# A tail of the first K block on a second DMA queue, and half as many wo rows for the first five DMA engines

## The chip, the cores and the metric

One core of a Trainium2 chip runs the whole kernel. The metric is the device time in microseconds (us) of one execution; medians are given with their range. The **span** of a profile runs from the first to the last instruction and is some 1.8 us shorter than the time of the same run.

## The reference

Attention of 4 new tokens in each of 8 sequences over a cache of 2048 keys, with 32 query heads and 8 key/value heads, between two projections:

```python
B, Sq, D = 8, 4, 512;  Hq, Hkv, Sk, Dh = 32, 8, 2048, 128
q = (x @ wq).reshape(B, Sq, Hq, Dh) ...
scores = einsum("bhqd,bhkd->bhqk", q, repeat(k_cache, 4)) * Dh ** -0.5
o = einsum("bhqk,bhkd->bhqd", softmax(scores), repeat(v_cache, 4))
return o... @ wo                       # everything bf16
```

K and V caches are 32 MB each, wq and wo 4 MB each: every byte is read once, so the kernel streams some 75.5 MB.

## The kernel before

The cache is cut into 32 units of 1 MB for K and 32 for V. All loads go on the sync queue, in the order K block 0, wq, x, then K and V blocks, with eight small loads of wo rows strewn in, and the rest of wo last.

```python
def load_k(u):
    ...
    nc.sync.dma_start(ks[u][:, :, :],
        k_cache[b, 2 * p : 2 * p + 2].rearrange("g (s c) d -> (g s) c d", c=C))   # 128 rows of 8 KB

NE, WE, WM, WN = 40, 8, 5, 64          # wo rows of the first 1024: NE*WE + 128*WM + WN

def load_wo_e(i):                      # five partitions x 8 rows of wo (8 KB each), i = 0..7
    ...
    nc.sync.dma_start(wo_e[a : a + 17 : 4, :, :], rows[b : b + 17 : 4, :, :])

load_k(0)
nc.sync.dma_start(wq_sb[:, :, :], wq.rearrange("(p r) n -> p r n", r=R))         # 128 rows of 32 KB
nc.sync.dma_start(x_sb[:, :], x.flatten_outer_dims())
loads = []
for u in range(NU + KA):
    if 1 <= u <= 8:
        loads.append(("e", u - 1))     # a five-row wo load between two K blocks
    if 0 < u < NU:
        loads.append(("k", u))
    ...                                # "v" blocks; wo_m and wo_n near the end
```

A load of five rows runs on five DMA engines alone (engines 0 to 4, by the rule that the prediction below cites). That looks intended: 320 wo rows are ballast for these engines. Why they should need it, the trace doesn't tell, since its packet records don't name the engine. The program's tool chain gives each DMA a semaphore on which its landing is counted; there are eight of them, used over and over.

The softmax here doesn't subtract the row's maximum and nothing guards it: scores larger than these inputs give would overflow.

## Time and profile before

| | before |
|---|---|
| time, median of 3 (range) | 188.69 us (188.62 to 189.28) |
| span of the profiled run | 186.8 us |
| bytes on the sync queue, share of 16 DMA engines | 75.55 MB, 96.5% |
| busy: PE, DVE, ACT | 77%, 71%, 33% |
| wq's packets | 4.98 to 14.83 us |

How to read it: a row of digits is the busy share of each fortieth of the span in tenths, `DMA` the mean over the 16 DMA engines and `GB/s` what they moved. An issue line of the timeline gives start and duration of the instruction that *hands out* a transfer; the transfer itself comes later. "Landing" is the increment of the transfer's semaphore, one for each DMA engine that takes part, so 16 landing records of one load tell how far the engines are apart. A load on fewer engines has one record more, soon after its issue: the first wo_e load, issued at 4.26 us, has one at 5.50 and five at 15.47 to 15.63.

### The profile page before, as it was taken

The numbers are of one execution on the slowest core, as the hardware profiler recorded it, in microseconds if no ns is written. First come the engines' busy times: TensorE is split into PE (matmuls) and PEld (weight loads), VectorE is DVE, ScalarE is ACT, GpSimd is POOL, SyncE is SP. The second block draws the span as 40 slices with busy tenths as digits, with TensorE's granted clock in tenths as the row PEclk, the third lists the DMA queues.
The fourth block names the chain that finished last, engine by engine and source line by source line (L and its number), as shares of the span: only waits on it lengthen the run. The fifth ranks groups of instructions, "written<-read, shape, count | busy, mean of one in ns | idle before, by whom it ended". The sixth has DMA issues, their size and how long they took to land.

```text
span 186.8 us, 4854 instructions
## 1 busy us (share of the span) xinstructions
PE 143.7 (77%) x2090; PEld 115.0 (62%) x2090; DVE 131.9 (71%) x260; ACT 62.4 (33%) x110; POOL 4.6 (2%) x9
## 2 busy tenths in 40 slices
PE   0704789979989969999687878977676787987592
PEld 0701248867777757887666656866565666776471
DVE  0850278979797888888786873988686887798220
ACT  2021147344535343343333331533333332335000
POOL 8100000000000000000000000000000000000000
PEclk9999999999999999999999996999999998799659
DMA  5998999999999999999999999999999999999980
GB/s 198 475 449 372 423 437 428 419 423 421 432 423 423 425 430 426 418 428 428 430 418 426 428 421 423 425 423 428 425 428 421 426 421 432 425 422 404 417 315 11
DMA packets 10980, 75.86 MB, mean 406 GB/s; under 512 B 1288, under 2 KB 1448, under 8 KB 2600
## 3 DMA queue, kind: packets, MB, share of 16 engines
q1 hardware_dynamic: 10912, 75.55, 96.5%
q8 instruction: 16, 0.26, 0.5%
q14 instruction: 4, 0.03, 0.0%
q10 hardware_dynamic: 48, 0.02, 0.0%
HBM read 75.53 MB, written 0.03 MB: 405 GB/s over the span
## 4 chain that ended last, share of the span: by engine, by line
DMA 96%; PE 1%; SPq 0%; issue 0%; ACT 0%
DMA k_sb<-in_k_cache_dram 58%; DMA v_sb<-in_v_cache_dram 26%; DMA wq_sb<-in_wq_dram 8%; DMA wo_sb<-in_wo_dram 4%; PE kp L215 1%; SPq L118 0%; PE s_ps L286 0%; PE out_ps L480 0%; ACT out_sb L545 0%; SPq L128 0%
## 5 line engine op out<-in xcount | busy, mean ns | idle before, releaser
L215 PE MATMUL kp<-ident,k_sb 128*128 128x128 f32 x512 | 73.1, 291 | 22.5 <-DMA k_sb<-in_k_cache_dram 22.3
L215 PEld LDWEIGHTS kp<-ident,k_sb 128*128 128x128 f32 x512 | 59.5, 149 | 33.2 <-issue 18.9
L216 DVE COPY kt<-kp 128x1024 bf16<-128x1024 bf16 x96 | 63.0, 686 | 22.7 <-PE kp L215 22.4
L306 DVE STREAM_TRANSPOSE probs<-s_sb 64x512 bf16<-64x512 bf16 x64 | 44.9, 702 | 0.6
L296 ACT ACTIVATE s_sb<-s_ps 128x512 bf16<-128x512 f32 x32 | 19.1, 597 | 66.7 <-PE s_ps L286 65.2
L216 ACT COPY kt<-kp 128x1024 bf16<-128x1024 bf16 x32 | 32.4, 1012 | 16.3 <-PE kp L215 16.3
L343 PE MATMUL o_ps<-probs,v_sb 128*128 128x32 bf16 x640 | 19.2, 177 | 3.2 <-DMA v_sb<-in_v_cache_dram 2.2
L343 PEld LDWEIGHTS <-v_sb 128*128 128x128 bf16 x640 | 18.6, 96 | 4.3 <-DMA v_sb<-in_v_cache_dram 3.9
L286 PE MATMUL s_ps<-kt,q_bd 128*32 128x256 bf16 x512 | 21.2, 283 | 0.0
L286 PEld LDWEIGHTS <-q_bd 128*32 128x32 bf16 x512 | 10.8, 96 | 6.0 <-issue 4.7
L381 PE MATMUL o_ps<-v_sb,probs 128*64 128x256 bf16 x192 | 11.6, 274 | 0.0
L381 PEld LDWEIGHTS <-probs 128*64 128x64 bf16 x192 | 10.0, 110 | 0.9 <-issue 0.8
L401 ACT ACTIVATE o_sb<-o_ps,r_sb 128x256 f32<-128x256 f32 x6 | 2.8, 474 | 12.4 <-DVE r_sb L399 12.4
L354 DVE TENSOR_TENSOR oT<-o_ps,r_sb 128x32 bf16<-128x32 f32 x20 | 3.8, 191 | 3.6 <-PE o_ps L343 3.0
L296 ACT ACTIVATION_READ_ACCUMULATOR s_sb<-s_ps 128x1 f32 x32 | 6.2, 194 | 0.0
L336 DVE RECIPROCAL r_sb<-l_ps 128x64 f32<-128x64 f32 x10 | 5.6, 557 | 0.3
L410 PE MATMUL f_ps<-fold,o_sb 128*128 128x64 f32 x24 | 4.0, 287 | 2.4 <-ACT o_sb L401 2.4
L480 PE MATMUL out_ps<-wo_sb,oP 128*32 128x256 bf16 x48 | 5.0, 342 | 0.5 <-DMA wo_sb<-in_wo_dram 0.5
L252 DVE COPY qT_all<-qtp 128x128 bf16<-128x128 bf16 x8 | 1.2, 217 | 5.8 <-PE qtp L246 5.8
L410 PEld LDWEIGHTS f_ps<-fold,o_sb 128*128 128x128 f32 x24 | 3.1, 190 | 3.6 <-ACT o_sb L401 3.3
L227 PE MATMUL xtp<-ident,x_sb 32*128 32x32 bf16 x4 | 0.3, 194 | 6.3 <-DMA x_sb<-in_x_dram 6.3
L243 ACT ACTIVATE q_nat<-psq 128x512 bf16<-128x512 f32 x2 | 1.2, 597 | 10.4 <-PE psq L236 10.4
(59 smaller groups left out, 64.1 us busy)
## 6 DMA issues: line engine op xcount, KB each, us to landing
k_sb<-in_k_cache_dram SPq DMA_DIRECT2D x32, 1024.0 KB, 19.6
v_sb<-in_v_cache_dram SPq DMA_DIRECT2D x32, 1024.0 KB, 12.6
wq_sb<-in_wq_dram SPq DMA_DIRECT2D x1, 4096.0 KB
wo_sb<-in_wo_dram SPq DMA_DIRECT2D x4, 512.0 KB
wo_sb<-in_wo_dram SPq DMA_DIRECT2D x4, 256.0 KB, 9.3
wo_m<-in_wo_dram SPq DMA_DIRECT2D x1, 640.0 KB, 16.7
wo_e<-in_wo_dram SPq DMA_DIRECT2D x8, 40.0 KB
wo_n<-in_wo_dram SPq DMA_DIRECT2D x1, 64.0 KB
```

The lines of the kernel that those rows point to most:

```text
L215: nc.tensor.transpose(kp[:, j, :], k4[:, w : w + 128], ident4[:, :])
L216: (nc.scalar.copy if part == 3 else nc.vector.tensor_copy)(out=kt[(u, t)][:, half * JT // 2 : (half + 1) * JT // 2, :, :].rearrange("k j s ...
L286: nc.tensor.matmul(s_ps[y * 32 : (y + 1) * 32, t * JT : (t + 1) * JT, :], lhsT=q_bd[:, p, e, b, y // 2, :, :], rhs=kt[(u, t)][:, :, y * 32 ...
L296: nc.scalar.activation(out=s_sb[:, :, :], in_=s_ps[:, :, :], func=EXP, accum_out=l_sbs[u][:, u % 2 : u % 2 + 1],)
L306: nc.vector.transpose(out=pr[rows, :, g, :], in_=s_sbs[u][rows, :, :].rearrange("q j s -> q (j s)"))
L336: nc.vector.reciprocal(r_sb[:, :, :], l_ps[:, :, :])
L343: nc.tensor.matmul(o_ps[:, :], lhsT=vs[u][:, c, :], rhs=pr[:, c, :, :].rearrange("s g q -> s (g q)"), start=(c == 0), stop=(c == C - 1),)
L354: nc.vector.tensor_tensor(out=oT[(p + 1) // 2][:, :, (p == 2) * 1, b, :], in0=o_pss[u][:, :].rearrange("d (h s) -> d h s", h=HP), in1=r_sb ...
L381: nc.tensor.matmul(o_ps[i * 64 : (i + 1) * 64, :], lhsT=probs[(u + i) % len(probs)][:, c : c + 2, :, :].rearrange("s c g q -> s (c g q)"), ...
L401: nc.scalar.mul(out=o_sb[:, :, :].rearrange("q c d -> q (c d)"), in_=o_ps[:, :], mul=r_sb[:, 0:1])
L410: nc.tensor.matmul(f_ps[:, :, :].rearrange("d u q -> d (u q)"), lhsT=o_sbs[u][:, c, :], rhs=fold[:, c, :, :].rearrange("k u q -> k (u q)") ...
L480: nc.tensor.matmul(out_ps[half * T : (half + 1) * T, :], lhsT=o, rhs=w[:, half * DH : (half + 1) * DH], start=(p == 0 and r == 0), stop=(p ...
```

## The change

Two things are meant to make the sixteen DMA engines end together. First, 160 instead of 320 rows of wo go through the first five engines (four loads instead of eight); wo_m grows from 5 to 6 rows per partition and wo_n from 64 to 96 rows. Second, the last two of the 32 chunks of K block 0 (512 B in each of 128 rows) leave the first K load and go on the scalar queue in sixteen small loads of 15, 14, ... 1 and 8 rows. By the rule that the prediction cites, a load of k rows (k up to 15) uses the first k engines, so engine 0 gets 16 rows, engine 1 fifteen, and engine 15 none: a fine slope.

```diff
-    NE, WE, WM, WN = 40, 8, 5, 64
+    NE, WE, WM, WN = 20, 8, 6, 96
...
-        nc.sync.dma_start(
-            ks[u][:, :, :],
-            k_cache[b, 2 * p : 2 * p + 2].rearrange("g (s c) d -> (g s) c d", c=C),
-        )
+        rows = k_cache[b, 2 * p : 2 * p + 2].rearrange("g (s c) d -> (g s) c d", c=C)
+        if u > 0:
+            nc.sync.dma_start(ks[u][:, :, :], rows)
+            return
+        nc.sync.dma_start(ks[u][:, : C - 2, :], rows[:, : C - 2, :])
+        a = 0
+        for k in [*range(15, 0, -1), 8]:
+            nc.scalar.dma_start(ks[u][a : a + k, C - 2 :, :], rows[a : a + k, C - 2 :, :])
+            a += k
...
-        hi, m = divmod(i, 4)
         rows = wo[: NE * WE, :].rearrange("(q r) j -> q r j", r=WE)
-        a, b = hi * 32 + m, hi * NE // 2 + m
-        nc.sync.dma_start(wo_e[a : a + 17 : 4, :, :], rows[b : b + 17 : 4, :, :])
+        nc.sync.dma_start(wo_e[i : i + 17 : 4, :, :], rows[i : i + 17 : 4, :, :])
...
-        if 1 <= u <= 8:
+        if 1 <= u <= 4:
```

The cut parts give wo_e 32 partitions instead of 64, one copy fewer on DVE in the reordering of the outputs, and one more row of wo_m in the projection.

More of the change, by code (lines that the diff above doesn't have):

```diff
@@ L74 @@
     pad0 = const.tile([128, 192], BF16, name="pad0")
-    wo_e = const.tile([64, WE, D], BF16, name="wo_e")
+    wo_e = const.tile([32, WE, D], BF16, name="wo_e")
     wo_n = const.tile([WN, D], BF16, name="wo_n")
@@ L92 @@
     oP12 = const.tile([128, WR, 2, T], BF16, name="oP12")
-    nat_sb = const.tile([2 * T, HP * 128 + 24 * WE], BF16, name="nat_sb")
+    nat_sb = const.tile([2 * T, HP * 128 + 12 * WE], BF16, name="nat_sb")
     oP3 = const.tile([128, WR, T], BF16, name="oP3")
     oP = [None, oP12[:, :, 0, :], oP12[:, :, 1, :], oP3[:, :, :]]
-    oE = const.tile([64, WE, T], BF16, name="oE")
+    oE = const.tile([32, WE, T], BF16, name="oE")
     oM = const.tile([128, WM, T], BF16, name="oM")
@@ L105 @@
     ones = const.tile([128, 128], FP32, name="ones")
-    pad = const.tile([128, 64], BF16, name="pad")
+    pad = const.tile([128, 128], BF16, name="pad")
     probs = [const.tile([128, C, 2, HQ], BF16, name=f"probs{i}") for i in range(3)]
@@ L431, in to_tokens @@
         flat = nat[:, :, :].rearrange("t h d -> t (h d)")
-        nats[n] = nat_sb[:rows, : HP * 128 + (n == 0) * 24 * WE]
+        nats[n] = nat_sb[:rows, : HP * 128 + (n == 0) * 12 * WE]
         if n > 0:
@@ L438, in to_tokens @@
         nc.vector.tensor_copy(out=nats[0][:, :w], in_=flat[:, :w])
-        nc.vector.tensor_copy(
-            out=nats[0][:, w : 2 * w], in_=flat[:, NE // 2 * WE : NE // 2 * WE + w]
-        )
-        nc.vector.tensor_copy(out=nats[0][:, 2 * w :], in_=flat[:, NE * WE :])
+        nc.vector.tensor_copy(out=nats[0][:, w:], in_=flat[:, NE * WE :])
     def to_wo_rows(n):
@@ L455, in to_wo_rows @@
         perm = psum_l.tile([128, WE + WM + 1, T], BF16, tag="l", name="perm")
-        w = 64 * WE
+        w = 32 * WE
         by_row = nats[0][:, :w].rearrange("t (q r) -> t r q", r=WE)
         for r in range(WE):
-            nc.tensor.transpose(perm[:64, r, :], by_row[:, r, :], ident[:T, :T])
+            nc.tensor.transpose(perm[:32, r, :], by_row[:, r, :], ident[:T, :T])
         by_row = nats[0][:, w : w + 128 * WM].rearrange("t (q r) -> t r q", r=WM)
@@ L464, in to_wo_rows @@
         nc.vector.tensor_copy(out=oN[:, :], in_=perm[:WN, WE + WM, :])
-        nc.vector.tensor_copy(out=oE[:, :, :], in_=perm[:64, :WE, :])
+        nc.vector.tensor_copy(out=oE[:, :, :], in_=perm[:32, :WE, :])
         nc.vector.tensor_copy(out=oM[:, :, :], in_=perm[:, WE : WE + WM, :])
```

## The prediction

> **What bounds the kernel now.** I read the strip of forty slices first, then the table of DMA queues, then the chain that ended last.
>
> ```profile
> DMA  5998999999999999999999999999999999999980
> GB/s 198 475 449 372 423 437 428 419 423 421 432 423 423 425 430 426 418 428 428 430 418 426 428 421 423 425 423 428 425 428 421 426 421 432 425 422 404 417 315 11
> ...
> q1 hardware_dynamic: 10912, 75.55, 96.5%
> q8 instruction: 16, 0.26, 0.5%
> ...
> DMA 96%; PE 1%; SPq 0%; issue 0%; ACT 0%
> ```
>
> The 16 DMA engines are full from the second slice to the last but two; 75.55 MB on one queue take 96.5% of their time, and 96% of the final chain is transfers. PE (77%) and DVE (71%) have slack. So the time is: when the engines start streaming, plus the work of the most loaded engine, plus a tail. Splitting the span into stretches gives 1.00 DMA share and 418 GB/s from 15.3 to 183.3 us. Any idle time of the DMA engines at the front is therefore not won back later.
>
> Two more views matter. First, the sync queue's issues at the start (start, duration):
>
> ```profile
> 0.73 0.39 SPq L118 DMA_DIRECT2D k_sb<-in_k_cache_dram  x1
> 1.19 0.42 SPq L151 DMA_DIRECT2D wq_sb<-in_wq_dram  x1
> 1.65 0.43 SPq L152 DMA_DIRECT2D x_sb<-in_x_dram  x1
> 4.26 0.84 SPq L138 DMA_DIRECT2D wo_e<-in_wo_dram  x1
> 5.16 0.40 SPq L118 DMA_DIRECT2D k_sb<-in_k_cache_dram  x1
> 5.60 0.72 SPq L138 DMA_DIRECT2D wo_e<-in_wo_dram  x1
> 6.36 0.43 SPq L118 DMA_DIRECT2D k_sb<-in_k_cache_dram  x1
> 6.84 0.42 SPq L128 DMA_DIRECT2D v_sb<-in_v_cache_dram  x1
> 7.31 0.70 SPq L138 DMA_DIRECT2D wo_e<-in_wo_dram  x1
> 15.33 0.34 SPq L118 DMA_DIRECT2D k_sb<-in_k_cache_dram  x1
> ```
>
> wq goes out at 1.19, right behind the first K block, so the engines pass from one to the other without a gap: in the packet records the first K packet starts at 2.43, the last ends at 5.15, and the first wq packet starts at 4.98. Second, the sync queue's own waits:
>
> ```profile
> SPq L128 <- DMA v_sb<-in_v_cache_dram: 47.4, 22, 3.1
> SPq L118 <- DMA k_sb<-in_k_cache_dram: 43.8, 22, 2.1
> ...
> SPq L118 <- DMA wq_sb<-in_wq_dram: 7.3, 1, 7.3
> ```
>
> A load of K waited 7.3 us for **wq** to land, though it doesn't read wq. The operands of the issues explain it: all DMAs take their completion semaphore from one ring of eight in program order, and each issue waits for the landing of the DMA eight before it. The issue at 15.33 is the tenth, wq the second. The two output DMAs at the end, one on the scalar and one on the sync queue, take two successive places of the same ring, the scalar one first, as in the source. So **the ring is shared by both queues**. At present that is harmless, because eight DMAs of mostly 1 MB cover any wait.
>
> **What the Trainium skill says.** (1) "DMA: Bandwidth & Descriptors", section "Why a DMA increments its semaphore by 16 and not by 1": a DMA runs on the largest k up to 16 that divides its slowest dimension, on the lowest-numbered k engines. The trace agrees: each five-row wo_e load has five landing records, each 128-row load sixteen. Groups of 15 down to 1 rows thus put 512 B on each of the first 15 down to 1 engines. (2) Same page, "Anatomy of one DMA — SWDGE (gpsimd) path": a semaphore wait happens on the issuing sequencer, before dispatch; the DMA engines never wait. The trace agrees: the 7.3 us above are the queue's. (3) Same page, "Issuing engines are not separate DMA queues": issuing from several engines saves only sequencer time. So the scalar queue brings no bandwidth. No run here shows that yet.
>
> **The change, part by part.**
>
> *wo rows (intended gain).* In the landing records of the last load the engines finish from 179.04 to 183.26 us. Sorted, their lags are three at 0 to 0.18, eleven at 2.49 to 2.98 or 3.09, one at 3.29 and one at 4.21; the mean is 2.46. The end waits for the one at 4.21. The lag grew in steps: eight wo_e loads at 8192 B, 0.309 us each, put 2.5 us on engines 0 to 4; the 16 instruction fetches of 16 KB (0.88 to 1.14 us each in the packet records) hit single engines for the rest. When the wo_e loads have landed (near 50 us) five engines stand out at 2.5 to 3.4, so the last one is most likely a wo_e engine that was also hit. The change takes four wo_e loads (32 KB) from each of engines 0 to 4 and gives every engine 8 KB more of wo_m and 2 KB of wo_n. The K tail takes 4 KB from every engine's part of the first block, and the triangle gives back between 8 KB (engine 0) and nothing (engine 15); that part is moved in the idle time found below. The rest is -26 KB for engines 0 to 4 and +6 KB for the others; at 8 KB per 0.306 us, -0.97 and +0.22 us. The slowest falls from 4.21 to 3.24, the others rise to about 3.2 or 3.3: **-0.9 us** at the end, more being impossible since the mean is hardly moved.
>
> *Sixteen small loads on the scalar queue.* Each has at most 15 rows of 512 B; the bytes (64 KB) are nothing. Their issue is not. A five-row issue takes 0.70 us against 0.33 to 0.42 for 128 rows; the output DMA took 0.394 us on scalar and 0.356 on sync. With the gap of 0.05 seen between issues I take 0.77 us apiece: 16 x 0.77 = 12.3 us of scalar queue from 0.73 to 13.0. Scalar's first data instruction (the last quarter of the first K transpose) ran at 9.31; it moves to about 14, still before x and wq, on which the next work waits. By itself hidden.
>
> *The ring.* The first K load is number 1, the sixteen are 2 to 17, **wq becomes number 18** and must wait for number 10, the ninth scalar load. That starts at about 0.73 + 8 x 0.77 = 6.9 us. (Its eighth must wait for the first K block, landed by 5.5, and starts at 6.1, so no delay there.) From issue to first packet took 1.70 us for the first K block and 0.93 for the scalar output DMA; I take 1.5, nearer the load. From the last packet to the landing it was 0.34 us for K. So the ninth lands at 6.9 + 1.5 + 0.05 + 0.34 = 8.8. Then wq is issued, its first packet at 8.85 + 1.5 = 10.35 instead of 4.98: **+5.4 us** with the engines idle but for the small rows. With the short latency it is 9.2 us (+4.2), with the long one and a 0.80 pitch about 11.1 (+6.1). The loads after wq wait for scalar loads 10 to 16, each 0.77 us later, up to about 14; wq keeps the engines busy for 9.8 us, so these are hidden.
>
> *Other parts.* One fewer copy on DVE, narrower oE, two more matmuls of wo_m/wo_n: DVE and PE have slack and these lie before the last loads land. 0.
>
> Sum: 188.69 + 5.4 - 0.9 = 193.2, or 192.0 to 193.9 over the two latencies. I put **193.0**.
>
> **Rivals.** *A: the gap does not open* (wq takes another semaphore, or is issued before the scalar loads). Then only the balance counts: 188.69 - 0.7 = 188.0, a "same". For it: somebody meant the triangle as a gain, and a 5 us gap would have been seen. Against: eight semaphores in strict program order over 80 issues and both queues. I give it 15%. *B: scalar becomes the bound.* If each small issue took over 1 us, or the activation table load of 1.28 us stood ahead of the issues instead of behind them, the ninth would land 1.3 to 2 us later: 194.5 or more. The load is now the first thing on scalar, but belongs to the first copy's line, so I expect it behind. 12%. *C: everything hidden anyway*, because compute makes up for a late start. It would need idle DMA time later on; the strip shows none, so no.
>
> **Range and chances.** Given the ring, the time lies around 193.0 with a spread of about 0.9, and the border of 2% slower is 192.46: some 75% of it is above. With A at 15%: slower 0.66, same 0.33, faster 0.01. Range 191.4 to 194.8.
>
> **What the changed profile would show.** The wq issue starts near 9 us instead of 1.19, and the sync queue's waits name it behind a k_sb landing for some 7 us; sixteen scalar issues about 0.77 us apart; the second of the forty slices drops well below 9 tenths DMA; the last wo_sb lands near 187.7 with the engines' spread at about 3.3 us instead of 4.2; the share of 1.00 in the long stretch stays. If wq is issued near 1.2, the ring argument is wrong and the time is about 188. If wq's issue is near 9 but the time grew by less than 4 us, the latency or the balance term is mis-sized. If PE waits for the first K block push x's transposes past wq's landing, the scalar issue was dearer than I took it.

## The result, and the profile after

| | before | after |
|---|---|---|
| time, median of 4 (range) | 188.66 us (188.35 to 189.28) | 193.56 us (192.86 to 194.41) |
| ratio of fast runs, 95% interval | | 1.0258 (1.0209 to 1.0307) |
| span of the profiled run | 186.8 us | 191.7 us |
| wq's packets | 4.98 to 14.83 us | 4.54 to 14.88 us |
| lags of the engines at the last wo load: largest, mean | 4.21, 2.46 us | 3.37, 1.89 us |
| last wo_sb landing | 183.26 us | 188.11 us |

A ratio here is the mean time of a kernel's fast runs over the mean of the other's fast runs of the same rounds, so not quite the ratio of the medians. The four runs after are fast, and no run before lies more than 0.5% above the fastest.

The time is near the predicted 193.0, 4.9 us more than before, and the loss lies at the start of the run. But the place of the loss is not the predicted one. The strip of slices after:

```profile
DMA  6992999999999999999999999999999999999980
GB/s 219 442 427 42 374 400 427 426 427 421 427 421 433 419 422 436 421 424 427 422 426 427 419 429 426 424 422 429 421 431 421 424 427 427 422 427 395 416 334 27
...
q10 hardware_dynamic: 304, 0.08, 0.2%
```

The second and third slice (4.8 to 14.4 us) are full: wq streams. The hole is the **fourth**, 14.4 to 19.2 us, with 42 GB/s. Slices five and six are full but slower, 374 and 400 GB/s; from slice seven on the strip looks as before. The last line is the scalar queue: 304 packets and next to no bytes. The issues of the sync queue and of the scalar queue in the same stretch (start, duration):

```profile
0.73 0.37 SPq L124 DMA_DIRECT2D k_sb<-in_k_cache_dram  x1
1.16 0.42 SPq L156 DMA_DIRECT2D wq_sb<-in_wq_dram  x1
16.20 0.34 SPq L157 DMA_DIRECT2D x_sb<-in_x_dram  x1
16.65 0.83 SPq L143 DMA_DIRECT2D wo_e<-in_wo_dram  x1
17.53 0.40 SPq L120 DMA_DIRECT2D k_sb<-in_k_cache_dram  x1
```

```profile
0.73 16.17 ACTq L127 DMA_DIRECT2D k_sb<-in_k_cache_dram  x16
16.93 1.28 ACT L221 ACT_TABLE_LOAD   x1 [16.93 <-DMA k_sb<-in_k_cache_dram]
```

wq goes out at 1.16, as early as ever. It is **x**, the next on the sync queue, that stands from 1.6 to 16.20, with everything behind it. The sixteen scalar issues, which I had put at 0.77 us each, take 16.17 us in all. The waits of the sync queue, in the first 30 us, name the culprit:

```profile
SPq L157 <- DMA k_sb<-in_k_cache_dram: 14.6, 1, 14.6
```

The load of x waits 14.6 us for a piece of K. It reads no K. It waits for a semaphore that a scalar load holds. What that costs the engines is seen by cutting out the stretch from wq's last packet to K block 1 (stretch; length; busy PE, PEld, DVE, ACT, POOL; clock; DMA share; GB/s), before and then after:

```profile
14.90:18.20 3.30, 2.21 (x20) 0.66 (x20) 0.22 (x1) 0.05 (x1) 0.00 (x0) 1.00 1.01 425
```

```profile
14.90:18.20 3.30, 0.06 (x1) 0.10 (x1) 0.00 (x0) 1.27 (x1) 0.00 (x0) 1.00 0.05 14
```

### The semaphores' places

The operands of the issues tell which semaphore each uses and waits for. Numbering the places in the ring of eight in the order in which they were given out: scalar load of 15 rows is 1, K block 0 is 2, scalar loads of 14 to 10 rows are 3 to 7, **wq is 8**, scalar loads of 9, 8, 7, 6, 5, 4, 3, 2, 1 and 8 rows are 9 to 18, x is 19, wo_e 20, K block 1 is 21, wo_e 22, K block 2 is 23, V block 0 is 24. So the ring is shared by both queues, but the order is not the source order across the queues: wq came early into it. x waits for place 11, the scalar load of 7 rows, whose last landing is at 16.18 us; x is issued at 16.20. The scalar load of 2 rows (16) waits for wq (8) itself.

### Why a scalar load of 3.5 KB lands at 16 us

The packet records of the scalar queue, which no view prints one by one, show the rhythm. While wq streams, the rows of successive scalar loads start at 5.76, 8.20, 10.65 and 13.10 us, and the small packets that increment the semaphore at 6.99, 9.44, 11.89 and 14.33. Rows and semaphore alternate, 1.22 or 1.23 us apart, which is the length of one wq packet (32 KB, 1.213 us). On each engine the scalar queue gets one turn after each wq packet, the row takes one turn and its semaphore write another: **2.45 us for a load of 27 ns of data**. The records don't name the engine; that this is a rhythm of each engine is read from the spacing. Six loads were issued before the first wait. The seventh waits for the first, the eighth for K block 0 (issues at 3.74 and 5.47 us), and the ninth to the eleventh for predecessors that land at this pace (7.92, 10.39 and 12.81 us). When wq ends at 14.9, the rest run at 0.2 to 0.4 us apiece, but by then the engines have nothing else to do.

### The profile page after: what moved, and what is told of

It reads as the page before. It is cut to its first block, busy times and chain, and to the rows that moved or that the text cites. A ratio compares the mean times of both kernels' runs of the same rounds, so it can differ in the third digit from the quotient of the medians.

```text
span 191.7 us, 4876 instructions
## 1 busy us (share of the span) xinstructions
PE 143.7 (75%) x2093; PEld 114.6 (60%) x2093; DVE 132.3 (69%) x259; ACT 62.4 (33%) x110; POOL 4.6 (2%) x9
## 4 chain that ended last, share of the span: by engine, by line
DMA 82%; PE 10%; DVE 2%; ACTq 2%; ACT 1%; issue 1%
DMA k_sb<-in_k_cache_dram 69%; DMA v_sb<-in_v_cache_dram 9%; PE kp L220 5%; DMA wo_sb<-in_wo_dram 4%; PE psq L241 2%; ACTq L127 2%; PE s_ps L291 2%; DVE probs L311 1%; PE qtp L251 1%; ACT q_nat L248 1%; PE pse L265 1%; DVE q_bd L274 0%; DVE kt L221 0%; DVE qT_all L257 0%; PE perm L452 0%
## 5 line engine op out<-in xcount | busy, mean ns | idle before, releaser
L348 PE MATMUL o_ps<-probs,v_sb 128*128 128x32 bf16 x640 | 19.2, 177 | 2.0 <-DVE by_gq L322 1.1
```

The source lines that it names most:

```text
L348: nc.tensor.matmul(o_ps[:, :], lhsT=vs[u][:, c, :], rhs=pr[:, c, :, :].rearrange("s g q -> s (g q)"), start=(c == 0), stop=(c == C - 1),)
```

## The experiments

Nine further kernels were run, two of them twice, and the changed kernel again as a control: twelve runs. The packet records allow a second reading beside the time. For each profile I took three numbers: when the last wo packet ended; the idle time of a DMA engine up to there (mean of 16); and the time that packets took beyond the usual for their size (0.309 us for 8 KB, 1.213 for 32 KB and so on; mean of 16), called slow packets. The two columns are differences to the kernel before. They need not add up to the difference in the last wo packet, since the first block's packets do not all start together (the earliest at 1.7 to 1.8 us in every profile, others up to 2.7) and packets overlap a little. How these two are counted moves the last two columns by up to 0.3 us.

| run | what | median us (range) | ratio, 95% interval | last wo packet | idle | slow packets |
|---|---|---|---|---|---|---|
| kernel before | | 188.66 (188.35 to 189.28) | 1 | 182.96 | 0 | 0 |
| kernel after | | 193.56 (192.86 to 194.41) | 1.0258 (1.0209 to 1.0307) | 187.83 | +4.0 | +1.3 |
| e11_after_again | the same again | 193.62 (193.17 to 193.95) | 1.0231 (1.0183 to 1.0279) | 187.73 | +4.2 | +0.7 |
| e1_rows | wo rows alone | 188.01 (187.69 to 190.10) | 0.9965 (0.9910 to 1.0021) | 182.34 | -0.7 | +0.2 |
| e2_tail | scalar loads alone | 193.55 (193.26 to 194.21) | 1.0243 (1.0182 to 1.0303) | 187.44 | +3.6 | +0.9 |
| e3_scratch | scalar loads into an unread tile | 193.17 (193.09 to 193.57) | 1.0215 (1.0164 to 1.0266) | 187.95 | +3.6 | +1.3 |
| e4_one | tail in 1 scalar load | 188.13 (188.00 to 189.98) | 0.9967 (0.9907 to 1.0027) | (profile of the 189.98 us run) | | |
| e12_four | tail in 4 | 188.68 (187.95 to 195.14) | 0.9963 (0.9900 to 1.0026) | 182.44 | -0.4 | +0.3 |
| e5_eight | tail in 8 | 190.90 (190.12 to 191.44) | 1.0098 (1.0030 to 1.0165) | 185.51 | +1.1 | +1.7 |
| e9_eight_again | the same again | 190.66 (189.78 to 190.91) | 1.0067 (1.0018 to 1.0116) | 185.18 | +0.6 | +1.5 |
| e6_wq8k | 16 scalar loads, wq in 8 KB packets | 191.62 (190.38 to 193.07) | 1.0144 (1.0050 to 1.0239) | 186.19 | +1.1 | +1.9 |
| e10_wq8k_again | the same again | 191.65 (191.47 to 192.55) | 1.0139 (1.0084 to 1.0193) | 186.13 | +1.2 | +2.1 |
| e7_sync | 16 loads on the sync queue | 194.77 (193.15 to 199.31) | 1.0280 (1.0140 to 1.0419) | 187.90 | +4.1 | +1.0 |
| e8_rows_wq8k | wo rows, wq in 8 KB packets | 188.07 (187.77 to 190.85) | 0.9949 (0.9909 to 0.9988) | (slow profile) | | |

All were correct. Ranges hold all runs, ratios fast ones only. Two runs of e12_four (191.58 and 195.14), one of e7_sync and one of e8_rows_wq8k were slow; in the rounds of e12_four one of eleven runs of the kernel before was slow too, and one of 191.34 counts as fast. The rounds of e5 to e8 were the worst, with four of eight runs of the kernel before slow.

**The theory** after reading the trace: the loss is wholly the scalar loads; they hold places of the ring for which x, wo_e and the next K loads must wait, and they give them up late because they take turns with 32 KB packets. **Rivals:** the rows cost part of it; the late last quarter of K block 0 delays the compute and so the loads; the mere number of small loads costs its share each; splitting the first block costs by itself.

### e1_rows and e2_tail: each half of the change alone

```diff
 e1_rows = after, with K block 0 whole on the sync queue
 e2_tail = before, with the sixteen scalar loads
```

> The new split of wo rows alone (160 through the first five engines), first K block whole on the sync queue. Theory (ring of eight semaphores plus slow small loads makes the whole loss): no gap behind wq, so 187.8 to 188.5 us, a gain of 0.2 to 0.9 from the smaller lag of the slowest engine (4.21 us before). My predicted balance term was -0.9; the changed kernel's lags (max minus mean 1.48 us against 1.75) suggest only -0.3. Rival (the rows themselves cost part of the +4.9, for instance through the larger wo_m late in the run): above 189.5 us.

> The sixteen scalar loads alone, wo rows as before. Theory: the whole loss, 193.3 to 194.5 us, with DMA engines idle for about 4 us from 15 to 19 us. Rival (loss shared with the rows): under 192 us.

The rows alone gave 188.01 us against 188.84 of the kernel before in the same rounds. The ratio 0.9965 has an interval that includes 1, so the gain by itself is not shown to be real by this run; the packet records agree with it, though (last wo packet 0.6 us earlier, with 0.7 us less idle time). The scalar loads alone gave 193.55 us: the whole loss. Rows as the cause are out. Nor does a gain of the rows show beside the loads: 193.55 us without them, 193.56 and 193.62 with them.

### e3_scratch: is it the data, or the semaphores?

```diff
-        nc.sync.dma_start(ks[u][:, : C - 2, :], rows[:, : C - 2, :])
+        nc.sync.dma_start(ks[u][:, :, :], rows)
-            nc.scalar.dma_start(ks[u][a : a + k, C - 2 :, :], rows[a : a + k, C - 2 :, :])
+            nc.scalar.dma_start(idle[a : a + k, :, :], rows[a : a + k, C - 2 :, :])
```

> As the changed kernel, but the first K block is loaded whole on the sync queue and the sixteen scalar loads go to a tile that nothing reads. Theory (the loads that follow wq on the sync queue wait for semaphores that the scalar loads hold): unchanged, 193 to 194.2 us, gap from 15 to 19 us as before. Rival (the compute chain is late because the first K block's last quarter lands at 18.0 us instead of 5.5, and that delays buffers and loads): the data are there at 5.5 us, so about 188.3 us.

193.17 us: as the theory has it. Nobody reads the scalar loads' data, K block 0 is complete at 5.7 us, and the loss is still there. The sync queue's issues and its waits in the first 25 us:

```profile
3.83 0.33 SPq L157 DMA_DIRECT2D wq_sb<-in_wq_dram  x1
14.50 0.34 SPq L158 DMA_DIRECT2D x_sb<-in_x_dram  x1
16.28 0.84 SPq L144 DMA_DIRECT2D wo_e<-in_wo_dram  x1
17.17 0.40 SPq L121 DMA_DIRECT2D k_sb<-in_k_cache_dram  x1
```

```profile
SPq L158 <- DMA idle<-in_k_cache_dram: 10.3, 1, 10.3
SPq L157 <- DMA idle<-in_k_cache_dram: 2.7, 1, 2.7
SPq L144 <- DMA idle<-in_k_cache_dram: 1.4, 1, 1.4
```

x, wq and wo_e all wait for the tile that nobody reads. In this kernel wq itself had to wait as well (its place is now the first scalar load's), but only until 3.83, while K block 0 was still streaming, so its first packet came only 0.2 us later (5.21 us against 4.98). Its first packets were slow, though (up to 1.97 us instead of 1.213), and its last ended at 15.80 instead of 14.83 us, so about 1 us of this kernel's loss lies before the end of wq and not behind it. A late K block as the cause is out.

### e4_one, e12_four, e5_eight and its repeat: how many places

```diff
-        for k in [*range(15, 0, -1), 8]:                       # sixteen loads
+        nc.scalar.dma_start(ks[u][:, C - 2 :, :], rows[:, C - 2 :, :])        # e4_one
+        for a in range(0, 128, 32): nc.scalar.dma_start(ks[u][a : a + 32, ... # e12_four
+        for a in range(0, 128, 16): nc.scalar.dma_start(ks[u][a : a + 16, ... # e5_eight
```

> The same 64 KB tail on the scalar queue as ONE load of 128 rows of 512 B. Theory: one place of the ring and about 2 to 20 us behind wq's packets but nobody but the first K block waits for it: 187.8 to 188.8 us. Rival (splitting the first K block over two queues or 512 B rows cost by themselves): 190 us or more.

> As the changed kernel, but the tail goes in eight scalar loads of 16 rows instead of sixteen. Theory (the ring of eight is what couples them): the loads behind wq then wait for scalar loads 2 to 4, which land during wq (7.9 to 12.8 us in the changed kernel) and not after it, so hardly a gap: 188 to 189.3 us. Rival (each small load costs its share of the loss, 0.3 us): 190.8 us.

> Repeat of e5_eight, whose rounds fell on a chip on which half the runs of the kernel before were in the slow state, and whose profile shows K packets of up to 2.6 us at 15 to 19 us that no other profile has. Theory (ring): with undisturbed runs 188 to 189.3 us. Rival (a share of the loss for each small load): 190.8 us again.

> As the changed kernel, but the tail goes in four scalar loads of 32 rows. With one load the time was 188.1 us, with eight 190.7, with sixteen 193.6. Theory (the loads behind wq are late only if the scalar loads they wait for land after wq's last packets): with four, the places that x, wo_e and the next two K loads wait for are free by 12.5 us, before wq ends, so no loss: 187.9 to 188.5 us, idle DMA time below 0.7 us. Rival (every small load costs some 0.35 us wherever it is): 189.1 to 189.3 us.

One load: 188.13 us; neither a second queue nor 512 B rows cost anything by themselves. Eight loads: 190.90 and again 190.66 us. My expectation was 188 to 189.3, and the rival's 190.8 was hit exactly. So at this point the rival "a share for each load" led. With four loads it wants 189.1 to 189.3; the runs in the fast state were 187.95, 188.36, 188.57 and 188.78 (mean 188.41), about as with one load. Going by the fast runs, then, **the cost is not an equal share for each load: it sets in between four loads and eight**. The median of all six, 188.68, is higher because two runs were slow. The sync queue of e12_four (wo_e issues left out):

```profile
1.62 0.43 SPq L155 DMA_DIRECT2D x_sb<-in_x_dram  x1
5.14 0.40 SPq L120 DMA_DIRECT2D k_sb<-in_k_cache_dram  x1
9.20 0.34 SPq L120 DMA_DIRECT2D k_sb<-in_k_cache_dram  x1
12.93 0.33 SPq L133 DMA_DIRECT2D v_sb<-in_v_cache_dram  x1
```

K block 2 and V block 0 do wait for scalar loads (issued at 9.20 and 12.93, against 6.36 and 6.84 before), but three blocks are queued before wq ends, so no engine runs dry. The pace fits the turns: a load of 32 rows has two rows and one semaphore write for each engine, three turns, and the two issues that wait for successive loads are 3.73 us apart (three wq packets are 3.64). With eight loads (e9_eight_again):

```profile
7.96 0.34 SPq L155 DMA_DIRECT2D x_sb<-in_x_dram  x1
10.44 0.84 SPq L141 DMA_DIRECT2D wo_e<-in_wo_dram  x1
12.86 0.36 SPq L120 DMA_DIRECT2D k_sb<-in_k_cache_dram  x1
15.38 0.72 SPq L141 DMA_DIRECT2D wo_e<-in_wo_dram  x1
16.15 0.44 SPq L120 DMA_DIRECT2D k_sb<-in_k_cache_dram  x1
```

Here my expectation went wrong by an oversight: I had followed the waits for scalar loads 2 to 4 only, up to K block 1. The wo_e load behind it waits for the fifth, which lands at 15.36, after wq. The queue is in order, so K block 2 goes out at 16.15, and one block (8 packets of 0.309 us for each engine, 2.5 us) is all that stands behind wq. That makes a gap of only 0.2 us (mean of the engines, 16.5 to 19 us); another 0.3 us of idle time lies directly behind wq (14.5 to 16.5 us), where K block 1 had been handed out 2 us before. The larger part of this kernel's loss is something else: the packets of K block 1, at 15 to 19 us, are slow, up to 2.6 us for 8 KB instead of 0.309, together 1.4 us per engine between 10 and 20 us in both profiles.

### e6_wq8k, its repeat and e8_rows_wq8k: the length of a turn

```diff
-    nc.sync.dma_start(wq_sb[:, :, :], wq.rearrange("(p r) n -> p r n", r=R))    # packets of 32 KB
+    nc.sync.dma_start(wq_sb[:, :, :], wq.rearrange("(r p) n -> p r n", r=R))    # packets of 8 KB
 (x is cut in the same way, so the product is the same)
```

> As the changed kernel with all sixteen scalar loads, but wq is read with rows (r p) instead of (p r): packets of 8 KB (0.31 us) in place of 32 KB (1.21 us), same bytes, still one load. Theory (a small scalar load gets one turn per packet of wq on each engine, two turns per load, hence 2.45 us apart): the scalar loads land some 0.6 us apart, all but the last few before wq does, and the gap closes: 188 to 189.5 us. Rival (the number of loads and of ring places alone makes the loss): 193 us as before.

> Control for e6_wq8k: new wo rows, first K block whole, wq in 8 KB packets, no scalar loads. Expected as with the rows alone, 187.7 to 188.5 us: the packet size of wq by itself does not matter while one queue is in use. If it is slower by more than 1 us, e6_wq8k must be compared with this one and not with the kernel before.

> Repeat of e6_wq8k for the same reason. Its profile had 1.7 us of idle DMA time against 4.6 in the changed kernel, part of it near 21 us, where a V load waited for the scalar load that waited for wq. Theory (turns behind wq's packets make most of the loss): 189 to 190.2 us undisturbed, some 3 to 4 us under the changed kernel of the same rounds. Rival (ring places alone): equal to the changed kernel.

The turn is confirmed: in e6_wq8k scalar loads 2 to 5 now land first at 6.12, 6.76, 7.40 and 8.03 us, **0.64 us apart** instead of 2.45, two turns of an 8 KB packet (0.309 us). The sync queue of e6_wq8k from x on (wo_e issues left out; those of the repeat lie within 0.2 us of these):

```profile
11.41 0.35 SPq L157 DMA_DIRECT2D x_sb<-in_x_dram  x1
13.10 0.36 SPq L120 DMA_DIRECT2D k_sb<-in_k_cache_dram  x1
14.53 0.43 SPq L120 DMA_DIRECT2D k_sb<-in_k_cache_dram  x1
20.25 0.33 SPq L135 DMA_DIRECT2D v_sb<-in_v_cache_dram  x1
```

x and K blocks 1 and 2 go out before wq ends; the great hole after wq is gone, and mean idle time fell by 3 us against the changed kernel. The time fell by 2 us only (191.65 against 193.62 in the same rounds). Both expectations were missed: 188 to 189.5 by 2.1 us, and 189 to 190.2 for the repeat by 1.4. What is left has two parts. V block 0 waits for the scalar load of 2 rows and so comes at 20.25 only, which leaves a second, smaller gap near 21 us. That load was issued at 15.99, as soon as wq had landed, but its rows started at 19.45 us (19.66 in the repeat), 3.5 us later, while K packets of 8 KB streamed. One turn after each packet does not explain that wait, and no run tells what does. And again slow packets, 1.8 us per engine between 10 and 30 us in the repeat, against none before. The control without scalar loads took 188.07 us: wq's packet size alone costs nothing.

### e7_sync: the gap that was predicted, made on purpose

```diff
-            nc.scalar.dma_start(ks[u][a : a + k, C - 2 :, :], rows[a : a + k, C - 2 :, :])
+            nc.sync.dma_start(ks[u][a : a + k, C - 2 :, :], rows[a : a + k, C - 2 :, :])
```

> As the changed kernel, but the sixteen tail loads go on the sync queue, ahead of wq. Here the gap that the prediction put ahead of wq must open: sixteen issues of about 0.35 us, half of them held until the first K block lands at 5.4 us, so wq is issued near 8 us and the engines idle for 3 to 4 us from 5 us on: 191 to 192.5 us. If the time is below 189.5 us, neither issue time nor the ring counts on one queue; if above 193, the small loads cost more than their issue.

```profile
1.17 7.30 SPq L127 DMA_DIRECT2D k_sb<-in_k_cache_dram  x16
8.51 0.36 SPq L156 DMA_DIRECT2D wq_sb<-in_wq_dram  x1
```

On one queue wq does come last of the eighteen, is issued at 8.51, and its first packet starts at 9.48 us, 4.5 us later than in the kernel before. That is 0.97 us after its issue. The runs took 193.15 and 193.49 us, a third fast one 196.04, above the 191 to 192.5 that I expected here; idle time grew by 4.1 us where I had put 3 to 4. So a delay of wq of about the size that I predicted costs about what I predicted, but it occurs only in this kernel; the sixteen issues took 7.30 us with half of them held until K block 0 had landed, so 0.3 to 0.5 us apiece, not 0.77.

## Why the prediction was right, and where it was not

The number was right, and so was half of the mechanism: that the kernel cannot win back idle DMA time at the start, and that the small loads hold places of a shared ring. The path from there to the loss was another one.

- **DMA-bound, and a front-end loss is not won back: right.** From 29 us on (slice seven) both kernels stream alike, and what was lost until then is in the end time: last wo_sb landing 183.26 to 188.11, +4.85, time +4.9.
- **A ring of eight semaphores shared by both queues: right.** The operands and e3_scratch show it: waits for a tile that nobody reads.
- **"wq becomes number 18": wrong.** The places are not given out in source order across the queues. wq took place 8 and was issued at 1.16. The load that paid was x (place 19), and with it all that follows in order. The predicted sign "the wq issue starts near 9 us" did not appear; its waiting time went to x, 14.6 us instead of some 7. Rival A's condition (wq not held) was thus met, and its conclusion (188.0 us) was false all the same, and with it the sign "if wq is issued near 1.2, the ring argument is wrong and the time is about 188". The prediction had looked at the loads behind wq, and had taken their waits, "up to about 14", as hidden; x went out at 16.20, after wq's last packet.
- **The scalar loads' cost, 0.77 us each: wrong in kind.** The pure issue is 0.25 to 0.66 us. What makes them slow is the turn behind each 32 KB packet, two turns or 2.45 us per load, a step that the prediction did not have. It took these loads "by itself hidden"; the last of them landed at 18.05 us and not near 14, so PE's last transpose of K block 0 ran at 18.14, after wq had landed (15.5). This is the last sign that the prediction named, for a scalar issue dearer than assumed; it was the landing, though, and not the issue.
- **The sum, +5.4: near, by another path.** Against the +5.4 stand 4.0 us more idle time (mean of engines) and 1.3 us of slow packets. Both gaps come from the same sixteen loads in the same ring, but the one measured is set by wq's packet length. That two different gaps have about the same size is luck. Nor were the terms of the predicted one right: the first K packets start at 1.78 us (eight of them), not at 2.43, so the 1.70 us from issue to first packet was 1.05, and e7_sync shows 0.97 for wq. With 1.05 in place of 1.5 the prediction's own sum gives +4.5 and 192.3 us, under the border of 2%.
- **The balance, -0.9: likely right where there is no gap, and not seen in the changed kernel.** In e1_rows the largest lag is 3.20 us (predicted 3.24), and largest minus mean fell from 1.75 to 1.03; the rows alone ended 0.6 us earlier by packets and 0.8 us by medians. The runs of e1_rows alone do not exclude zero; with e8_rows_wq8k (0.9949, at most 0.9988, but with wq cut differently as well) it looks real. In the changed kernel the largest lag fell to 3.37, but the mean fell along with it, so largest minus mean improved by 0.3 us only (to 1.48), and e2_tail, with the old rows, was as fast (193.55 us). So the +4.9 is the loads' loss alone, and not 5.4 less 0.9.
- **Activation table load behind the issues: right**, at 16.93.
- **Small slips.** The five-row loads have six landing records and not five (see above), and 26 KB at 8 KB per 0.306 us are 0.99 us, not 0.97; neither matters for the sum.

**What stays open.** In every kernel whose stream behind wq was interrupted, K packets near the interruption were slow: 470 to 1260 ns for the first ones in the changed kernel, up to 2.6 us in e5_eight, and none in e1_rows or e12_four. In e7_sync it was wq's first packets after the gap (up to 2.5 us instead of 1.213). It is repeatable (e9_eight_again, e10_wq8k_again) and makes up most of the loss with eight loads. But the interruption is not shown to be the cause: with eight loads the slow packets begin at 14.8 to 15.1 us, directly behind wq, before the queue runs out of blocks and while the last four scalar loads land (15.0 to 16.5 us in e9_eight_again). No run separates the two. The slow packets in the profiles of e4_one (189.98 us) and e8_rows_wq8k (190.85) are of another kind: hundreds of 8 KB packets took 0.32 to 0.36 us and only one more than that, and nothing was interrupted. No run tells why either kind is slow. Nor was the direct test of the ring made, a kernel in which the scalar loads have semaphores of their own.

No version beat the kernel before by clearly more than 0.5%. The best are those without the sixteen loads: e1_rows and e8_rows_wq8k, 188.0 us. What the slope over the engines is worth, which the small loads were to give, was not measured apart from its cost of five microseconds.

## What to carry to other kernels

A small transfer was not cheap here for being small: it held a completion semaphore until it landed, and on the second queue it landed at the pace of the other queue's packets. Before adding many small loads at a place where few large ones are in flight, list who waits for their semaphores next, and count the loads against the ring. If they must be there, make them few (four were free here, eight were not), or put them where the neighbours' packets are short (8 KB instead of 32 KB won back 2 of the 5 us here).

## What the Trainium skill lacked or had wrong

- "DMA: Bandwidth & Descriptors", section "Queues, rings and completion order", says that an engine changes between queues at packet boundaries, typically after 9 to 17 descriptors. The turns are there, and the prediction did not use them. But here every turn beside wq was one packet record on either side: one row of wq of 32 KB, then one 512 B row of the scalar queue; and the row and its semaphore write took a turn each (1.22 and 1.23 us apart, 2.45 us per load; 0.64 us with 8 KB rows). Later the turns fail: beside K packets of 8 KB a load of two rows, issued at 15.99 us, had its first row at 19.45 (e6_wq8k).
- The same page, section "Issuing engines are not separate DMA queues", names only saved sequencer time as the effect of a second queue. It lacks the reverse: beside a stream of 32 KB rows, sixteen small loads kept the scalar queue for 16.17 us.
- No page says that semaphores which a tool chain shares between queues couple the queues: x on the sync queue waited 14.6 us for a scalar load that it did not need (10.3 us in e3_scratch, where nothing reads the loads at all).
- No page has the slow packets near an interruption of the stream: 8 KB in 0.5 to 2.6 us instead of 0.309, 0.7 to 2.1 us more per engine than in the kernel before.
